# Decode attention with a parallel MLP on one core: the fourth V group is loaded by seven transfers instead of one

## The chip, the cores and the metric

The kernel runs on one core of a Trainium2 chip. The metric is the device time of one execution in microseconds (us); lower is better. Three executions of the kernel before gave 101.88, 101.95 and 102.9 us, a median of 101.95 us. One further execution was recorded by the hardware profiler.

## The reference

One decode step (one token, model width 1024) goes through two branches, whose results are added to the token:

```python
xn = layernorm(x)                                  # 1 x 1024
# branch A: attention over the last W = 4096 positions
q = xn @ wq                                        # 32 heads of 128; wq is 1024 x 4096
k = k_cache[:, :, Sk - W:, :]                      # 4 groups of 4096 x 128, 8 query heads each
v = v_cache[:, :, Sk - W:, :]
p = softmax(q . k * 128 ** -0.5)
A = (p . v) @ wo                                   # wo is 4096 x 1024
# branch B: MLP
h = gelu_tanh(layernorm(xn) @ w1 + b1)             # w1 is 1024 x 3584
B = h @ w2 + b2                                    # w2 is 3584 x 1024
out = x + A + B
```

Everything is bf16. Each weight and each cached position is used for one token only, so the core has to bring in some 40 MB and does little arithmetic on each byte.

## The kernel before

The program is written with one instruction stream for each engine and explicit semaphores; no scheduler changes the order. All bulk loads are issued by the SP queue in the order of the source: four transfers of wq (2 MB each, into the tile WA), four of w1 (1.75 MB each, into the tile W1, which the profile calls W), four of K and four of V (1 MB each, one for each group, into the tile KV). Then SP waits until TensorE has read all of w1 (line 304), and issues four transfers of w2 into the place of w1 and seven of wo into the place of wq (line 140, in `load_rows`; the sizes are in `W2_CHUNKS` and `WO_CHUNKS`). ACT issues three loads of one row each at the start (x, b1 and b2).

Each bulk transfer covers all 128 partitions. In a V transfer (line 192) partition m of group g receives the positions 32 m to 32 m + 31, which lie next to each other in memory: one row of 32 x 128 bf16 elements, 8 KB. The transfer raises the semaphore `s_v[g]` by 16 when all its data has landed.

TensorE works through the stages in the order in which the data arrives: the q projection (line 267), the first MLP layer (line 282), transposes of K (line 360), scores (line 382), softmax with DVE and ACT, the first nine row blocks of w2 (line 422), then probabilities times V (line 445), the rest of w2, and wo (line 422 again, called from line 471). Ahead of line 445 it waits for all four V groups (line 442). After each wo transfer but the first and the last, some matmuls without use are run (line 473). The last wo matmul releases the copy on ACT (line 477) and the output write (line 479).

Of the kernel before, what the change touches and what calls it, by code (L numbers as in the profile page):

```python
# [13 lines left out]
DH = 128  # L14
REP = HQ // HKV
SK = 65536
W = 4096
NBLK = W // 128
# [4 lines left out]
W1_CHUNKS = [2, 2, 2, 2]  # L23
W2_CHUNKS = [9, 9, 8, 2]
WO_CHUNKS = [8, 8, 8, 4, 2, 1, 1]
KEEP_BUSY = [[], [512] * 6, [512] * 2, [512], [256], [256], []]
PAD = 32

# [13 lines left out]
def bass_parallel_sum__sliding_block_cached__mixer_channel_mlp__decode_kernel(  # L42
# [18 lines left out]
    pe, dve, act, pool, sp = nc.tensor, nc.vector, nc.scalar, nc.gpsimd, nc.sync  # L61

    def sems(name, n):
        return [nc.alloc_semaphore(f"{name}{i}") for i in range(n)]
# [5 lines left out]
    s_v = sems("s_v", HKV)  # L70
    s_wo = sems("s_wo", len(WO_CHUNKS))
    s_w2 = sems("s_w2", len(W2_CHUNKS))
# [46 lines left out]
    V = KV[:, HKV * W: HKV * W + HKV * NBLK * DH]  # L119
# [17 lines left out]
    def load_rows(dst, src, chunks, width, semaphores):  # L137
        c0 = 0
        for j, n in enumerate(chunks):
            sp.dma_start(  # L140
                dst[:, c0 * width:(c0 + n) * width].rearrange("p (c n) -> p c n", c=n),
                src[:, c0:c0 + n, :],
            ).then_inc(semaphores[j], 16)
            c0 += n
# [44 lines left out]
            A_k_cache[0, g, SK - W:SK, :].rearrange("(m b) d -> m (b d)", m=128),  # L189
        ).then_inc(s_k[g], 16)  # L190
    for g in range(HKV):
        sp.dma_start(
            V[:, g * NBLK * DH:(g + 1) * NBLK * DH],
            A_v_cache[0, g, SK - W:SK, :].rearrange("(m b) d -> m (b d)", m=128),
        ).then_inc(s_v[g], 16)


    def stats(src, ms, veps):
# [106 lines left out]
    load_rows(W2, w2_p, W2_CHUNKS, D, s_w2)  # L305
    load_rows(WA, wo_p, WO_CHUNKS, D, s_wo)

# [36 lines left out]
    for u in range(NUNIT):  # L344
        g, hu = u // 2, u % 2
# [71 lines left out]
    def out_rows_mms(weights, vec, chunks, semaphores, j, stop_at=None):  # L417
        c0 = sum(chunks[:j])
        pe.wait_ge(semaphores[j], 16)
        for c in range(c0, c0 + chunks[j]):  # L420
            for a in range(4):
                ins = pe.matmul(acc(a), lhsT=vec[:, c:c + 32],  # L422
                                rhs=weights[:, c * D + a * 256: c * D + (a + 1) * 256],
                                start=False, stop=(c == stop_at))
        return ins
# [13 lines left out]
    pe.wait_ge(ACT.sem, C["exp"])  # L439
    wait_kt(pe, 5)  # L440
    for g in range(HKV):
        pe.wait_ge(s_v[g], 16)
    V4 = V.rearrange("p (g b d) -> p g b d", g=HKV, b=NBLK)
    for b in range(NBLK):
        last = pe.matmul(PS[0:32, 4 * 512:5 * 512], lhsT=Pb[:, b * HQ:(b + 1) * HQ], rhs=V4[:, :, b, :],  # L445
# [23 lines left out]
    pe.wait_ge(DVE.sem, C["OT"])  # L469
    for j in range(len(WO_CHUNKS)):  # L470
        last = out_rows_mms(WA, OT, WO_CHUNKS, s_wo, j, stop_at=31)
        for n in KEEP_BUSY[j]:
            pe.matmul(PS[0:32, 0:n], lhsT=OT[:, 0:32], rhs=WA[:, 0:n])  # L473
# [37 lines left out]
```

## Time and profile before

| What | Value |
|---|---|
| median of three executions | 101.95 us |
| the profiled execution | 101.74 us |
| its span, from first to last instruction | 100.5 us |
| outside the span | 1.24 us |
| bytes moved, mean rate | 39.94 MB, 397 GB/s |
| TensorE matmuls busy | 70.4 us |
| DVE, ACT, GpSimd busy | 21.4, 12.0, 3.1 us |

The span is what the trace covers; the time of an execution has about 1.2 us more. The page cuts the span into 40 slices of 2.5 us. A digit for an engine or for the DMA is its busy share in tenths, with 9 for 90% or more. The core has 16 DMA engines; this text calls what one of them has to do for the SP queue a ring. Every row of a transfer is a packet in the trace, with its start, its duration and its size, and each ring ends its part of a transfer with a packet of 4 bytes that counts the semaphore up. The trace also has the moment of each such count, here called a landing mark: 16 marks for each 128-row transfer.

### The profile page before, as it was taken

The numbers are of one execution on the slowest core, as the hardware profiler recorded it, in microseconds if no ns is written. First come the engines' busy times: TensorE is split into PE (matmuls) and PEld (weight loads), VectorE is DVE, ScalarE is ACT, GpSimd is POOL, SyncE is SP. The second block draws the span as 40 slices with busy tenths as digits, with TensorE's granted clock in tenths as the row PEclk, the third lists the DMA queues.
The fourth block names the chain that finished last, engine by engine and source line by source line (L and its number), as shares of the span: only waits on it lengthen the run. The fifth ranks groups of instructions, "written<-read, shape, count | busy, mean of one in ns | idle before, by whom it ended". The sixth has DMA issues, their size and how long they took to land.

```text
span 100.5 us, 1606 instructions
## 1 busy us (share of the span) xinstructions
PE 70.4 (70%) x727; PEld 37.9 (38%) x727; DVE 21.4 (21%) x48; ACT 12.0 (12%) x15; POOL 3.1 (3%) x18
## 2 busy tenths in 40 slices
PE   0439999999795729576999856049997507098761
PEld 1322224344232213226999842035444404061430
DVE  0453000000200000029869344540005100000000
ACT  2206000000000000025547400400000000000001
POOL 6600000000000000000000000000000000000000
PEclk9999999999999999999999985555999996555899
DMA  4899999999999999999999999999999999999940
GB/s 105 352 441 450 424 417 424 430 431 428 439 417 412 428 445 399 423 427 421 421 417 414 424 437 451 433 404 445 407 409 445 417 430 437 430 417 395 397 154 1
DMA packets 3907, 39.94 MB, mean 397 GB/s; under 512 B 439, under 2 KB 443, under 8 KB 958
## 3 DMA queue, kind: packets, MB, share of 16 engines
q1 hardware_dynamic: 3896, 39.85, 94.6%
q8 instruction: 5, 0.08, 0.3%
q10 hardware_dynamic: 6, 0.01, 0.0%
HBM read 39.86 MB, written 0.00 MB: 397 GB/s over the span
## 4 chain that ended last, share of the span: by engine, by line
DMA 67%; SPq 26%; PE 4%; issue 1%; ACT 0%
DMA W<-in_B_w_dram 37%; DMA WA<-in_A_wo_dram 30%; SPq L140 26%; PE PS L282 3%; ACT ORow L477 0%; PE PS L422 0%; PE PS L291 0%
## 5 line engine op out<-in xcount | busy, mean ns | idle before, releaser
L267 PE MATMUL PS<-WA,XNZ 128*8 128x512 bf16 x64 | 16.4, 424 | 0.0
L282 PE MATMUL PS<-W,YTb 128*1 128x512 bf16 x56 | 12.7, 379 | 5.0 <-DMA W<-in_B_w_dram 5.0
L422 PE MATMUL PS<-WA,OT 128*32 128x256 bf16 x128 | 6.7, 355 | 8.6 <-DMA WA<-in_A_wo_dram 8.5
L267 PEld LDWEIGHTS PS<-WA,XNZ 128*8 128x8 bf16 x64 | 6.0, 94 | 10.8 <-issue 4.3
L282 PEld LDWEIGHTS PS<-W,YTb 128*1 128x1 bf16 x56 | 4.4, 83 | 13.4 <-DMA W<-in_B_w_dram 6.0
L422 PEld LDWEIGHTS PS<-WA,OT 128*32 128x32 bf16 x128 | 3.9, 121 | 12.3 <-DMA WA<-in_A_wo_dram 7.8
L360 PE MATMUL PS<-identb,KV 128*128 128x128 bf16 x128 | 7.5, 219 | 1.3 <-ACT ROW L295 1.3
L422 PE MATMUL PS<-W,GT 128*32 128x256 bf16 x112 | 5.2, 321 | 4.1 <-DMA W<-in_B_w_dram 4.1
L360 PEld LDWEIGHTS PS<-identb,KV 128*128 128x128 bf16 x128 | 7.2, 98 | 1.5 <-ACT ROW L295 1.4
L445 PE MATMUL PS<-KV,Pb 128*32 128x512 bf16 x32 | 7.6, 398 | 0.0
L367 DVE COPY KV<-PS 128x1024 bf16<-128x1024 bf16 x10 | 6.3, 686 | 0.6 <-PE PS L360 0.6
L372 ACT ACTIVATE KV<-PS 128x1024 bf16<-128x1024 bf16 x6 | 5.8, 1019 | 1.9 <-PE PS L360 1.9
L297 DVE CAST ROW<-PS 1x2048 bf16<-1x2048 f32 x1 | 2.3, 2278 | 17.1 <-PE PS L282 17.1
L295 ACT ACTIVATE ROW<-PS 1x1536 bf16<-1x1536 f32 x1 | 1.4, 1439 | 34.6 <-PE PS L282 34.6
L422 PEld LDWEIGHTS PS<-W,GT 128*32 128x32 bf16 x112 | 3.5, 110 | 5.2 <-DVE SUMP L409 4.6
L445 PEld LDWEIGHTS PS<-KV,Pb 128*32 128x32 bf16 x32 | 3.2, 102 | 4.0 <-issue 0.8
L274 DVE CAST Q<-PS 8x512 bf16<-8x512 f32 x1 | 0.7, 679 | 17.8 <-PE PS L267 17.8
L477 ACT ACTIVATE ORow<-PS 128x256 bf16<-128x256 f32 x1 | 0.4, 383 | 33.8 <-PE PS L422 33.8
L473 PE MATMUL PS<-WA,OT 128*32 128x512 bf16 (+1 forms) x11 | 4.3, 499 | 0.0
L382 PE MATMUL PS<-QT,KV 128*128 128x8 bf16 x128 | 3.4, 166 | 0.4 <-DVE KV L367 0.4
L382 PEld LDWEIGHTS PS<-QT,KV 128*128 128x128 bf16 x128 | 3.3, 96 | 0.6 <-DVE KV L367 0.6
L259 PE MATMUL PS<-ROW,oneb 1*1 1x512 bf16 x7 | 3.1, 619 | 0.0
(85 smaller groups left out, 34.0 us busy)
## 6 DMA issues: line engine op xcount, KB each, us to landing
WA<-in_A_wq_dram SPq DMA_DIRECT2D x4, 2048.0 KB, 14.0
W<-in_B_w_dram SPq DMA_DIRECT2D x4, 1792.0 KB, 30.6
WA<-in_A_wo_dram SPq DMA_DIRECT2D x3, 2048.0 KB, 39.1
W<-in_B_w_dram SPq DMA_DIRECT2D x2, 2304.0 KB, 24.7
KV<-in_A_k_cache_dram SPq DMA_DIRECT2D x4, 1024.0 KB, 39.4
KV<-in_A_v_cache_dram SPq DMA_DIRECT2D x4, 1024.0 KB, 34.1
W<-in_B_w_dram SPq DMA_DIRECT2D x1, 2048.0 KB, 31.7
WA<-in_A_wo_dram SPq DMA_DIRECT2D x1, 1024.0 KB, 42.2
```

The costliest lines, as they stand in the source:

```text
L140: sp.dma_start(dst[:, c0 * width:(c0 + n) * width].rearrange("p (c n) -> p c n", c=n), src[:, c0:c0 + n, :],).then_inc(semaphores[j], 16)
L259: pe.matmul(PS[0:1, t * 512:(t + 1) * 512], lhsT=oneb[:, :], rhs=B1R[:, t * 512:(t + 1) * 512], start=True, stop=False)
L267: last = pe.matmul(PS[0:8, 7 * 512:8 * 512], lhsT=XNZ[:, 15 * k + 7 - t:15 * k + 15 - t], rhs=WA[:, k * NQ + t * 512: k * NQ + (t + 1) * 512],
L282: last = pe.matmul(PS[0:1, t * 512:(t + 1) * 512], lhsT=YTb[:, k:k + 1], rhs=W1[:, k * F + t * 512: k * F + (t + 1) * 512], start=False, s ...
L297: C["d_hrow"] = DVE.mark(dve.tensor_copy(Hrow[:, 1536:F], PS[0:1, 1536:F]))
L360: last = pe.matmul(PSb[:, o:o + 128], lhsT=KT[:, col + bb * 128: col + (bb + 1) * 128], rhs=identb[:, :], is_transpose=True)
L367: C["dkt"][u] = DVE.mark(dve.tensor_copy(KT[:, col + 1024 * s: col + 1024 * (s + 1)], PSb[:, bk * 1024:(bk + 1) * 1024]))
L372: C["akt"][u] = ACT.mark(act.activation(out=KT[:, col + 1024: col + 2048], in_=PSb[:, bk * 1024:(bk + 1) * 1024], func=ACTF.Copy))
L382: last = pe.matmul(PS[:, b * HQ + g * REP: b * HQ + (g + 1) * REP], lhsT=KT[:, g * W + b * 128: g * W + (b + 1) * 128], rhs=QT[:, g * 8:(g ...
L422: ins = pe.matmul(acc(a), lhsT=vec[:, c:c + 32], rhs=weights[:, c * D + a * 256: c * D + (a + 1) * 256], start=False, stop=(c == stop_at))
L445: last = pe.matmul(PS[0:32, 4 * 512:5 * 512], lhsT=Pb[:, b * HQ:(b + 1) * HQ], rhs=V4[:, :, b, :], start=(b == 0), stop=(b == NBLK - 1))
L473: pe.matmul(PS[0:32, 0:n], lhsT=OT[:, 0:32], rhs=WA[:, 0:n])
```

## The change

The fourth V group is brought in by seven transfers, and the wait of TensorE ahead of line 445 counts the semaphore up to 16 for each transfer of the group (112 for the fourth, 16 for the others as before). The seven cover the 128 partitions once: 64 rows (every second partition from 0), 32 rows (every fourth from 1), 16 rows (every eighth from 3), then the partitions 7, 15, ... 127, in three transfers of five rows and one of one row. The place in the SP queue, the other groups, all destinations and all arithmetic are the same.

```diff
+V_ALL = [(0, 128, 1)]
+V_CUT = [(0, 128, 2), (1, 128, 4), (3, 128, 8), (7, 47, 8), (47, 87, 8), (87, 127, 8), (127, 128, 1)]
+V_ROWS = [V_ALL, V_ALL, V_ALL, V_CUT]
...
     for g in range(HKV):
-        sp.dma_start(
-            V[:, g * NBLK * DH:(g + 1) * NBLK * DH],
-            A_v_cache[0, g, SK - W:SK, :].rearrange("(m b) d -> m (b d)", m=128),
-        ).then_inc(s_v[g], 16)
+        v_rows = A_v_cache[0, g, SK - W:SK, :].rearrange("(m b) d -> m (b d)", m=128)
+        for lo, hi, step in V_ROWS[g]:
+            sp.dma_start(
+                V[lo:hi:step, g * NBLK * DH:(g + 1) * NBLK * DH], v_rows[lo:hi:step, :],
+            ).then_inc(s_v[g], 16)
...
     for g in range(HKV):
-        pe.wait_ge(s_v[g], 16)
+        pe.wait_ge(s_v[g], 16 * len(V_ROWS[g]))
```

## The prediction

> **What bounds the kernel.** I read the page's slices first, to see which resource is never idle.
>
> ```profile
> PE   0439999999795729576999856049997507098761
> DMA  4899999999999999999999999999999999999940
> DMA packets 3907, 39.94 MB, mean 397 GB/s; under 512 B 439, under 2 KB 443, under 8 KB 958
> q1 hardware_dynamic: 3896, 39.85, 94.6%
> q8 instruction: 5, 0.08, 0.3%
> q10 hardware_dynamic: 6, 0.01, 0.0%
> DMA W<-in_B_w_dram 37%; DMA WA<-in_A_wo_dram 30%; SPq L140 26%; PE PS L282 3%; ACT ORow L477 0%; PE PS L422 0%; PE PS L291 0%
> L422 PE MATMUL PS<-WA,OT 128*32 128x256 bf16 x128 | 6.7, 355 | 8.6 <-DMA WA<-in_A_wo_dram 8.5
> ```
>
> The DMA row is full from the third slice to the last but two, while TensorE has holes; in the last line TensorE waits 8.5 us for wo. So the end is set by the last byte of wo. The chain of waits, in order of time, gives the moments:
>
> ```profile
> 56.04 11.66 SPq L140
> 67.70 0.04 issue
> 67.75 30.27 DMA WA<-in_A_wo_dram
> 98.02 0.04 issue
> 98.06 0.32 PE PS L422 x4
> 98.41 0.38 ACT ORow L477
> ```
>
> The last wo transfer lands at 98.02, and 2.47 us follow it up to 100.49 (a matmul block, the copy, the write), which the change does not touch. The 26% that the chain puts on SP's issue is no bound: the next view, the timeline of SP, shows the last bulk issue over at 46.85 + 25.28 = 72.13, well ahead of its data.
>
> ```profile
> 17.42 16.45 SPq L192 DMA_DIRECT2D KV<-in_A_v_cache_dram  x4
> 44.52 2.29 SPq L140 DMA_DIRECT2D W<-in_B_w_dram  x4
> 46.85 25.28 SPq L140 DMA_DIRECT2D WA<-in_A_wo_dram  x7
> ```
>
> A transfer lands when the slowest of its 16 rings has finished, so I read the landing marks of the last one. They are not together: ten rings have 96.27 to 96.65, one has 96.82, and five have 97.78 to 98.02. The end therefore hangs on **five late rings**, 1.4 us behind the rest. They became late one by one: a single late mark in w1's third transfer (36.97 beside a median of 35.40), two in the second V group, five in the third wo transfer. The five instruction packets of q8 start at 31.17, 52.97, 59.83, 71.29 and 87.19 and take 1.02 to 1.08 each; each makes one ring late. The ring at 96.82 is another: its 0.3 us is there from the start, where the three one-row loads of q10 run (the first wq transfer has 15 marks up to 8.01 and one at 8.36).
>
> **The change part by part.** *Removed and added rows.* A V row is a packet of 8 KB that takes 309 to 312 ns; I take 310, and 9 ns for a 4-byte packet. The fourth group now costs every ring 8 x 310 + 9 = 2.49 us. How are fewer rows shared out? The output write of four rows has four data packets of 512 B and four landing marks of rings; a one-row load has one data packet and one. So five rows can use at most five rings, one row one ring. 64, 32 and 16 rows can use 16 rings with 4, 2 and 1 rows each. I take this, and that the small transfers begin at the same first ring each time; the one late mark that the three one-row loads leave together speaks for that. Then:
>
> - eleven rings have 7 rows and 3 counts: 7 x 310 + 27 = 2.20 us, 0.29 less than before;
> - four rings have 10 rows and 6 counts: 10 x 310 + 54 = 3.15 us, 0.66 more;
> - the first ring has 11 rows and 7 counts: 11 x 310 + 63 = 3.47 us, 0.98 more.
>
> [...]
>
> *What follows at the end.* Nothing behind V waits between the rings, so the differences stay until the last wo mark. The ten ordinary marks become at most 96.65 + 0.66 = 97.31. The ring of the one-row loads is the first ring: 96.82 + 0.98 = 97.80. The five late ones, if they lie among the eleven, become 98.02 - 0.29 = 97.73. The last of these is 97.80, 0.22 ahead of 98.02.
>
> *Price of a row in the small transfers.* No transfer of before writes a part of the partitions with a step, and none has rings that write where other rings write in a full transfer. Below I set 310 ns, as in full transfers; above 620, two packets one after the other on a shared way (the nearest row is a V-sized packet at 53.97 that met an instruction packet and took 856). I take 310, since full rows of 2, 4, 8, 14, 16 and 18 KB all run at 24 to 27 bytes per ns and ring, whatever their target. A gain over 310 is excluded: the same bytes never ran faster.
>
> [...]
>
> *Six more issues on SP* (the seven replace one). An issue that waits for nothing takes about 0.43 us there, those of V 3.7 to 4.6 because the queue is full. At 0.43 the six take 2.6 us, inside SP's idle time from 33.9 to 44.5. At 4.1 each they would take 25 us and pass it, so that the w2 issue begins near 58.5 instead of 44.5. Its data starts at 58.87 and an issue at 0.80 had its first packet at 1.82, so at the worst 0.7 us is lost. But the first nine issues of the run took 0.39 to 0.53 each and the tenth 3.52: an issue stalls only behind some nine queued transfers, so data remains in front. I take 0, ends 0 and 0.7. The w2 and wo issues queued behind have no other reader in a hurry: the last wo issue is over at 72.14, and the first 2 KB packet starts at 94.46.
>
> *TensorE's wait for 112* is hidden. The fourth group's last mark is 61.13; line 445 starts at 68.76, after the first w2 part (last mark 66.63), which is queued behind V. Even 4 us more keeps V first in the queue; without that cover, each late us would count once.
>
> *Sum:* -0.22 on the way to the last mark, 0 elsewhere: the profiled 101.74 becomes 101.52. The profiled run was 0.21 under the median of the runs, so the forecast is 101.95 - 0.22 = **101.73 us**. Since about 1% (1.0 us) is what a measurement of this kernel can tell from no change, this is "within 1%".
>
> **Rivals.** *Late rings under the small transfers.* If one of the five late rings is among the four that get 10 rows, its mark becomes 97.78 to 98.02 + 0.66 = 98.44 to 98.68, the end 0.4 to 0.7 later: **102.6** at the upper end. For it: the trace does not name rings. Against: the five instruction packets hit five different rings, as if taken in turn, and of the 11 runs of five neighbours that leave out the first ring, 7 leave out the next four as well.
>
> *Shared way of writing, the slower side.* One mechanism: in the seven transfers two rings write into one place at a time. If only the 16-row transfer and the single rows suffer, the first ring has 6 x 310 + 5 x 620 + 63 = 5.02, 2.53 more: its mark is 99.35 and the end 1.33 later, 103.3. If all rows do, 11 x 620 + 63 = 6.88, 4.39 more: 101.21, 3.19 later, 105.1. I price it at the middle, **104.2**. It decides above 1% when the first ring's rows take (98.02 + 1.02 - 96.82 + 2.49 - 0.06) / 11 = 0.42 us on average. For it: the full transfers leave the rings no spare time. Against: nothing in the trace shows two rings in each other's way.
>
> *The change doesn't shift the load.* If the small transfers take the rings in turn, 5 + 5 + 5 + 1 gives each ring one row, 8 as before, and a few counts more: +0.04, **102.0**. Against: the single late mark of the three one-row loads.
>
> *A dry queue* from the issues: +0.7 - 0.2, **102.5**.
>
> **How the numbers follow.** Forecast 0.38; late rings 0.17; shared way 0.36; no shift 0.05; dry queue 0.04. Faster by over 1% needs a loss of 1 us at the end, and the lightest ring only gains 0.29: 0.03 for what I don't see. Slower by over 1% is the shared way with most of its chance, 0.34, and 0.03 from sums of the others: 0.37. The rest, 0.60, is within 1%. The range begins at 101.4 (the five late rings' full 0.29, and the scatter of the runs) and reaches to 104.3, into the shared way's middle; the forecast with the other small cases alone has 101.4 to 102.7.
>
> **What the next profile would show.** Right: 4-byte packets of q1 grow from 436 by 16 + 16 + 5 + 5 + 5 + 1 = 48, landing marks of the last wo transfer with the five late ones 0.29 earlier and the first ring's near 97.8, V packets of 310 ns. The prediction is wrong if packets of the seven transfers take 420 ns or more, if a late mark moves 0.66 back, or if the DMA row has a hole near 60 us.

## The result, and the profile after

The changed kernel takes 102.89 us (median of ten runs, 102.76 to 103.46), the kernel before 101.88 us in the same comparison. The ratio is 1.0098, with an interval of 1.0078 to 1.0119: about 1.0 us slower. The forecast was 101.73 us, 0.2% faster. The range (101.4 to 104.3) holds the result; the direction was wrong.

The page after, the same rows as before. Its lines are numbered three to five higher (`load_rows` is line 143, the V loads line 197, the weight rows of w2 and wo line 426).

```profile
PE   0439999999896647759998934029999637088561
...
DMA  4999999999999999999999999999999999999940
GB/s 98 394 423 420 426 413 445 452 408 446 401 429 430 446 407 405 429 420 429 423 416 407 429 280 379 428 450 403 422 408 423 447 445 432 413 407 420 391 190 1
DMA packets 3955, 39.94 MB, mean 393 GB/s; under 512 B 487, under 2 KB 491, under 8 KB 1006
...
q1 hardware_dynamic: 3944, 39.85, 94.8%
q8 instruction: 5, 0.08, 0.3%
...
L426 PE MATMUL PS<-WA,OT 128*32 128x256 bf16 x128 | 6.5, 347 | 7.4 <-DMA WA<-in_A_wo_dram 7.3
```

The GB/s row of the page before, for comparison:

```profile
GB/s 105 352 441 450 424 417 424 430 431 428 439 417 412 428 445 399 423 427 421 421 417 414 424 437 451 433 404 445 407 409 445 417 430 437 430 417 395 397 154 1
```

The DMA engines are as busy as before, and the bytes are the same. What is new is in the GB/s row: the 24th slice, which begins at 58.4 us, has 280 (before 437), and the next has 379 (before 451). A busy share cannot show this, since a packet that is held up counts as busy (in the stretch shown next it is 1.07, before 1.03). The packets are 48 more, as predicted. TensorE waits no longer for wo than before (7.3 us, before 8.5): what it lost lies earlier, ahead of the first part of w2 (5.3 us, before 4.1).

The same by stretches of time: 58 to 63 us, in which the fourth V group and the first w2 transfer come in, and the rest. The last number is GB/s, the one ahead of it the DMA engines' busy share. First the kernel before, then the changed one.

```profile
58.00:63.00 5.00, 2.67 (x55) 1.74 (x51) 2.59 (x5) 0.00 (x0) 0.00 (x0) 0.66 1.03 434
63.00:98.00 35.00, 21.79 (x285) 12.01 (x285) 4.51 (x6) 1.02 (x1) 0.00 (x0) 0.76 0.96 402
```

```profile
58.00:63.00 5.00, 2.55 (x50) 1.62 (x47) 2.71 (x5) 0.00 (x0) 0.00 (x0) 0.70 1.07 343
63.00:98.00 35.00, 22.26 (x279) 12.10 (x280) 4.40 (x6) 1.02 (x1) 0.00 (x0) 0.70 0.98 414
```

Five us at 343 instead of 434 GB/s are 0.455 MB that did not move; at 434 GB/s that is 1.05 us, the whole loss. Behind 63 us nothing is lost. The chain of waits and SP's timeline agree: the last wo transfer lands 1.03 later than before (99.05, before 98.02), and the issues end early as before.

```profile
68.08 30.96 DMA WA<-in_A_wo_dram
99.05 0.04 issue
99.09 0.32 PE PS L426 x4
```

```profile
...
17.41 24.38 SPq L197 DMA_DIRECT2D KV<-in_A_v_cache_dram  x10
44.41 3.33 SPq L143 DMA_DIRECT2D W<-in_B_w_dram  x4
47.79 25.19 SPq L143 DMA_DIRECT2D WA<-in_A_wo_dram  x7
```

The packets of that stretch tell which ones were slow. The trace does not name rings, but each packet starts where the one before it on its ring ends (in the kernel before, the earliest marks of the four K transfers and the first V transfer, 41.98 to 51.92 us, stand 2.48 to 2.49 us apart, the length of eight packets of some 310 ns and one of 9), and the 4-byte packets part the transfers, so the rows can be followed. Between 54.3 and 58.5 us V packets take 309 to 340 ns, nearly as in full transfers; most rows of the 16-row transfer start there. All 23 V packets that start from 58.6 to 60.2 take 485 to 678 ns. Fifteen of them are single rows (485 to 593 ns), one is a row of the 16-row transfer, and seven are rows of the 64-row and 32-row transfers on the two rings that were already late then; the longest, 678 ns, is one of these. The 18 KB rows of w2 that start from 58.6 to 60.2 take 1.07 to 1.29 us instead of 0.69, and they belong to an ordinary transfer of 128 rows. So from 58.6 us on rows of every transfer under way are held up, and not only those of the small ones.

### The profile page after: what moved, and what is told of

Its sections match the earlier page's. It is cut to its first block, busy times and chain, and to the rows that moved or that the text cites. A ratio compares the mean times of both kernels' runs of the same rounds, so it can differ in the third digit from the quotient of the medians.

```text
span 101.5 us, 1612 instructions
## 1 busy us (share of the span) xinstructions
PE 71.8 (71%) x727; PEld 38.2 (38%) x727; DVE 21.2 (21%) x48; ACT 12.0 (12%) x15; POOL 3.2 (3%) x18
## 4 chain that ended last, share of the span: by engine, by line
DMA 67%; SPq 26%; PE 4%; issue 1%; ACT 0%
DMA W<-in_B_w_dram 36%; DMA WA<-in_A_wo_dram 30%; SPq L143 26%; PE PS L286 3%; ACT ORow L481 0%; PE PS L426 0%; PE PS L295 0%
## 5 line engine op out<-in xcount | busy, mean ns | idle before, releaser
L449 PE MATMUL PS<-KV,Pb 128*32 128x512 bf16 x32 | 9.0, 450 | 0.0
```

## The experiments

Three accounts were at hand. **A:** rows are merely dealt out to the wrong rings. **B:** a row that a ring writes into partitions that another ring writes in a full transfer shares a way with it, and both are slow (no trace names the partitions of a packet or a way, so this is the author's account of the numbers). **C:** every small transfer has a price of its own. Later **D:** the small transfers read badly, in rows of memory at a pitch of 64 KB.

**Which rings are late.** Fifteen tiny transfers of 1 to 15 rows behind the last wo transfer, in both kernels; in the changed one each of the seven transfers has its own semaphore too. (Here and below the cuts of code leave out the semaphores of added transfers and the waits for them at the end.)

```diff
+    for k in range(1, 16):
+        sp.dma_start(CEN[0:k, 32 * k - 32:32 * k], A_wo[0:k, 0:32]).then_inc(s_cen[k - 1], 16)
```

> The kernel before, with 15 tiny transfers of 1, 2, ... 15 rows of 64 bytes queued behind the last wo transfer, each with a semaphore of its own. A transfer of k rows uses k rings, so what is new in its landing marks beside those of k - 1 rows is the mark of ring k, and shows how late that ring is at the end. Theory A (late rings under the small transfers: the load is dealt out by rings and late rings are among those that got more rows): one or more of the five marks that are about 1.4 us late appear at k = 2 to 5. Theory B (shared way of writing): it leaves this open; if all five late marks appear at k = 6 or later, A falls. The first ring is expected 0.3 late in both.

> The changed kernel with a semaphore for each of the seven transfers and the same 15 tiny transfers at the end. Theory A: the rings 2 to 5 are 0.66 us later than in the kernel before, the first 0.98, the other eleven 0.29 earlier. Theory B: rings 1 to 5 are later by 1.3 to 2.5 us, and others, into whose partitions the 16-row and the single rows go, are later too, by 0.3 to 1 us, instead of earlier. Both expect about the time of the changed kernel, 102.9 us, or up to 0.3 more for the tiny transfers.

Measured: 101.84 and 103.19 us, one run each. The marks nest as expected: those of k rows are those of k - 1 rows some 0.19 later, and one new one. So each mark of the last wo transfer can be given to a ring:

| Ring | Last wo mark, before | after | moved by | row counts alone |
|---|---|---|---|---|
| 1 | 96.90 | 98.94 | +2.0 | +0.98 |
| 2 to 5 | 96.30 to 96.63 | 98.16 to 98.46 | +1.8 to +1.9 | +0.66 |
| 6, 7, 10, 11, 12 | 97.82 to 98.12 | 98.86 to 99.14 | +0.8 to +1.0 | -0.29 |
| 8, 9, 13 to 16 | 96.36 to 96.70 | 97.25 to 97.66 | +0.8 to +1.1 | -0.29 |

The five late rings are 6, 7, 10, 11 and 12. None is among those that got more rows, so A falls. The shift of rows took place as counted: the rings 2 to 5 moved about 0.9 more than the last eleven, where the counts say 0.95. But on top of it **every ring lost 1.1 to 1.4 us**. The sizes are about those that B gave: 1.3 to 2.5 us later for the rings 1 to 5, and 0.3 to 1 later for others instead of earlier. The last mark is that of ring 12, a late ring, which the prediction had gaining 0.29.

**Even numbers of rows.** Two cuts that give each ring eight rows again.

```diff
-V_CUT = [(0, 128, 2), (1, 128, 4), (3, 128, 8), (7, 47, 8), (47, 87, 8), (87, 127, 8), (127, 128, 1)]
+V_CUT = [(0, 128, 2), (1, 128, 4), (3, 128, 4)]                  # 64, 32, 32 rows
+V_CUT = [(0, 128, 2), (1, 128, 4), (3, 128, 8), (7, 128, 8)]     # 64, 32, 16, 16 rows
```

> Fourth V group by three transfers of 64, 32 and 32 rows (steps 2, 4 and 4; the last from partition 3): every ring has 8 rows again, no single rows. Theory A: no ring has more rows, so the time of before, 101.9 us (plus 0.02 for two more counts). Theory B, if only rows of the 16-row and single-row transfers share a way: also 101.9; if any step in the partitions makes rings share: 2.4 us more for these eight rows at 620 ns, 104.3. Theory C (each small transfer has a cost of its own to begin): 101.9 plus two such costs; the change's 1.0 us over six added transfers would be 0.17 each, so 102.2.

> Fourth V group by four transfers of 64, 32, 16 and 16 rows (steps 2, 4, 8 and 8, the last two from partitions 3 and 7): every ring has 8 rows, no single rows, but two transfers of 16 rows. Theory A: 101.9 us. Theory B: in each 16-row transfer two rings share a way, so that a row takes some 620 ns instead of 310: twice 0.31 more on all rings, 102.5. Theory C: three added transfers at 0.17, 102.4; B and C are told apart by the packets, which take 310 ns by C and some 500 to 620 by B.

Measured: 64, 32 and 32 rows have a ratio of 0.9998 (0.9976 to 1.0021), no change. With 64, 32, 16 and 16 rows it is 1.011 (1.0077 to 1.0143), 1.1 us and as much as the change itself, without any ring having more rows. The stretches of the first, then of the second:

```profile
58.00:63.00 5.00, 2.52 (x49) 1.59 (x46) 2.74 (x5) 0.00 (x0) 0.00 (x0) 0.64 1.05 442
```

```profile
58.00:63.00 5.00, 2.64 (x54) 1.71 (x51) 2.62 (x5) 0.00 (x0) 0.00 (x0) 0.74 1.06 359
```

442 beside 359 GB/s: cutting a transfer up and stepping over partitions cost nothing with 64 and 32 rows, whose V packets stay at 309 to 326 ns; two transfers of 16 rows do cost. That each ring keeps to its own partitions in the first cut and not in the second is B's reading; the trace does not name the partitions of a packet. The size was off: 0.62 had been expected from two rows at double time.

**Double dose.** The 16-row transfer is cut into 5, 5, 5 and 1 rows as well.

```diff
+V_CUT = [(0, 128, 2), (1, 128, 4), (3, 43, 8), (43, 83, 8), (83, 123, 8), (123, 124, 1), (7, 47, 8), (47, 87, 8), (87, 127, 8), (127, 128, 1)]
```

> The changed kernel with the 16-row transfer of step 8 also cut into 5 + 5 + 5 + 1 rows: 64, 32 and twice 5, 5, 5, 1. Now 11 rings have 6 rows and 5 or 6 have 12 to 14. By counts of rows alone the first ring, at 96.9 in the kernel before, would have 14 x 0.31 - 2.49 = 1.9 more, 98.8, so the end is 0.75 us later than before: 102.7. [...]

Measured: 103.89 us, ratio 1.0207 (1.0191 to 1.0224), 2.1 us over before, and 1.2 above what the counts of rows give (102.7).

**Where the rows are written, where they are read.** Back to the kernel before, with 384 KB more behind the fourth V group, into a scratch tile with 3 KB in each partition: by one transfer of 128 rows, or by eight of 16 rows, with the target or the source in two arrangements.

```diff
+    EX = sb("EX", [128, 1536], bf16)
+    sp.dma_start(EX[:, :], v_rows[:, 0:1536])                                  # one of 128 rows
+    for n in range(8):                                                         # eight of 16 rows:
+        sp.dma_start(EX[n:128:8, :], v_rows[n:128:8, 0:1536])                  # every eighth partition
+        sp.dma_start(EX[16 * n:16 * n + 16, :], v_rows[n:128:8, 0:1536])       # 16 neighbours
+        sp.dma_start(EX[n:128:8, :], v_rows[16 * n:16 * n + 16, 0:1536])       # every eighth, rows of memory neighbours
```

> The kernel before with 384 KB more: one transfer of 128 rows of 3 KB into a scratch tile, queued behind the fourth V group. It is the measure for the next two. Each ring gets 8 rows of some 0.12 us: about 1.0 us more than before (102.9), packets of some 120 ns, whatever the theory.

> The same 384 KB from the same memory rows into the same scratch tile, by eight transfers of 16 rows (every eighth partition). Theory B (two rings share a way into the partitions): rows take twice as long, 2.0 us more than before, 103.9. Theory C (each small transfer has a cost of its own, about 0.55 us after the kernel with two 16-row transfers): 1.0 + 8 x 0.55, 106.3, with packets of 120 ns and gaps between them. Theory D (the reading of 16 memory rows at a pitch of 64 KB is slow, wherever they go): the same time as the next one.

> Like the one with eight transfers of 16 rows, with the same memory rows in each transfer, but into 16 neighbouring partitions instead of every eighth. [...] Theories C and D: the same time as with every eighth partition.

> The kernel with eight 16-row transfers into every eighth partition, but each reads 16 neighbouring rows of memory (pitch 8 KB) instead of every eighth (64 KB). Theory D: now as fast as one transfer of 128 rows, 103.1. Theories B and C: as before with 64 KB, 104.6.

> The kernel with eight 16-row transfers into blocks of 16 neighbouring partitions, with the blocks in the order 0, 2, 4, 6, 1, 3, 5, 7 instead of 0 to 7; everything else the same. [...] Theory C (price for each small transfer) and theory D (reading at a pitch of 64 KB is slow): no change by the order, 104.7.

| Extra 384 KB | Ratio to before (interval) |
|---|---|
| one transfer of 128 rows | 1.0149 (1.0103 to 1.0195) |
| eight of 16 rows, every eighth partition | 1.0274 (1.0257 to 1.0291) |
| the same, neighbouring rows of memory | 1.0269 (1.0251 to 1.0286) |
| eight of 16 rows, 16 neighbouring partitions | 1.027 (1.0232 to 1.0307) |
| the same, blocks in the order 0, 2, 4, 6, 1, 3, 5, 7 | 1.0301 (1.0262 to 1.034) |

The one transfer of 128 rows already cost 1.5 us instead of the 1.0 expected. The source makes no difference, so D falls. C falls too: eight times 0.55 us would have been 106.3, and the packets themselves grow, from 121 ns in the 128-row transfer to some 240 in the 16-row ones. B's estimate for every eighth partition (103.9) was too low by 0.7, part of which lies in the 128-row transfer already. That blocks of 16 neighbours cost more than every eighth partition was the author's estimate, and no run shows it (1.027 beside 1.0274). The order of blocks is not settled by the times, since the intervals overlap. In the packets of the changed order the early blocks reach 416 ns, 3.4 times 121, and most later ones fall back to 210 to 260; in the order 0 to 7 nearly all stay under 250. The author's explanation, that the rings spread over several transfers and then meet less, is argued, not shown by a run of its own.

**The same transfers, 64 partitions higher.** Eight transfers of five rows of 3 KB use rings 1 to 5 and write the partitions 0 to 19 and 32 to 51, each transfer with a step of four; in the other kernel only the partitions differ, by 64. Which rings write the one or the other set in a full transfer no trace shows.

```diff
+    for n in range(8):
+        p = 0 + 32 * (n // 4) + n % 4      # 64 + ... in the other kernel
+        sp.dma_start(EX[p:p + 20:4, :], v_rows[n:n + 40:8, 0:1536])
```

> The kernel before with eight more transfers of five rows of 3 KB into a scratch tile behind the fourth V group: 24 KB more on each of the rings 1 to 5, as three rows of 8 KB in the change. [...] Theory B: no ring meets another; the first ring has 8 x 0.13 = 1.03 more and stays ahead of the late rings (96.9 + 1.03 = 97.9 beside 98.0): 101.9, no change. Theory C (price for each transfer): 0.17 each or more, 1.4 us on the rings 1 to 5 beside the 1.03: 99.3 on the first, 103.2. Theory D (pitch of 64 KB): as the next kernel.

> [...] By counts of rows alone, and by C and D: the time of the kernel with the partitions 0 to 51.

Measured: partitions 0 to 51 1.0005 (0.999 to 1.0021); 64 higher 1.0116 (1.0073 to 1.016). Same rings, same bytes, same memory rows, same number of transfers. First the rate with the partitions 0 to 51, then 64 higher:

```profile
58.00:63.00 5.00, 2.79 (x58) 1.86 (x54) 2.47 (x5) 0.00 (x0) 0.00 (x0) 0.51 1.05 436
```

```profile
58.00:63.00 5.00, 2.56 (x51) 1.64 (x47) 2.70 (x5) 0.00 (x0) 0.00 (x0) 0.73 1.05 359
```

With the partitions 0 to 51 all 40 packets take 121 ns. With those 64 higher they rise to 245, and the first w2 rows to 1.34 us. The time is 102.78, 0.9 over before. No mark of the first w2 transfer lies before 65.75, where with the partitions 0 to 51 the eight earliest lie from 64.84 to 65.20: taken in order, all 16 marks are 0.73 to 1.05 later. So rings that had nothing added are delayed too. For the same rows on the same rings, then, the time depended on the partitions they were written into. That agrees with B. Which rings meet was not shown, nor that in the partitions 0 to 51 none do.

**One ring alone, 64 partitions higher.** To see whether others are held up, the first ring alone writes 24 KB, into the partitions 0 to 3 and 32 to 35 or into those 64 higher.

```diff
+        sp.dma_start(EX[p:p + 1, :], v_rows[n:n + 1, 0:1536])      # p as above
```

> [...] The first ring has 8 x 0.13 = 1.0 more, 97.9 at the end, still ahead of the late rings: no change, 101.9; the other 15 rings' marks of the first w2 transfer as before (64.9 to 65.2 but for the three late ones).

> [...] If a contested way holds up every ring: all marks of the first w2 transfer move back together, by up to 1.0, the late ones too, and the time is 102.3 to 102.9.

Measured: partitions 0 to 35 1.001 (0.9992 to 1.0028), 64 higher 1.0034 (1.002 to 1.0049), about 0.3 us over before. The two intervals just overlap, so the times alone hardly tell the two apart; the spans do (100.4 to 100.8 us, and 100.8 to 101.1 with the higher ones), and so do the packets. First the stretch with the partitions 0 to 35, then 64 higher:

```profile
58.00:63.00 5.00, 2.67 (x55) 1.74 (x52) 2.59 (x5) 0.00 (x0) 0.00 (x0) 0.68 1.03 433
```

```profile
58.00:63.00 5.00, 2.78 (x59) 1.85 (x56) 2.48 (x5) 0.00 (x0) 0.00 (x0) 0.72 1.02 415
```

The rate of the stretch falls from 433 to 415 GB/s. On the writing ring the last 3 KB packets take 232 to 240 ns instead of 121. At the same time one other ring, which has nothing added, has two w2 rows of 1.12 and 1.10 us instead of 0.69, and one mark of the first w2 transfer stands alone at 65.83: a second ring is held up. Which one it is the trace does not name. A price of these partitions for the writing ring alone would not show on a second one. The last wo mark is 98.34 (98.08 with the partitions 0 to 35), on one ring alone (the next has 98.15); that it is the first ring was supposed and not shown. The other rings hardly move: eleven marks of the first w2 transfer lie from 64.92 to 65.20, beside 64.86 to 65.24 for the twelve earliest of before. Yet at 59.6 to 59.9 some w2 rows that had taken 686 to 694 ns take 720 to 729, on one ring after another. So here mainly two rings were slowed, and the others a little. With five rings writing 64 partitions higher (the pair of runs above) the earliest mark of that transfer is 65.75 instead of 64.84, and with the whole change all rings lost over 1.1. How the small hold grows into a loss on all rings stays open.

## Why the prediction was wrong

- **What bounds the kernel:** right. The last wo mark sets the end, and what was lost at 58 to 63 us came out undiminished at 99.05. TensorE's wait for the four V groups and the six issues cost nothing: the issues took 0.42 to 4.6 us each and ended at 41.8, inside SP's idle time.
- **How rows are dealt out:** right, with 48 more counts, k rows on k rings, always from the first ring (the nested marks show it), and none of the late rings among the first five. The last was partly luck: it had been argued from five neighbours hit in turn, and the late rings are 6, 7, 10, 11 and 12. The shift between the two sets of rings is there, about 0.9 us for 0.95.
- **The price of a row:** this step failed. The forecast took 310 ns for each row of the small transfers, "since full rows of 2, 4, 8, 14, 16 and 18 KB all run at 24 to 27 bytes per ns and ring, whatever their target", and put at nothing what these rows do to other rings. All of those transfers covered 128 partitions, so they could not speak about transfers that reach only a part of them. In its place the runs showed single rows of 485 to 593 ns, and rows of other transfers held up beside them: 1.07 to 1.29 us for a w2 row of 0.69. The first ring moved 2.0 us back where 0.98 was counted. The late rings, which set the end, moved 0.8 to 1.0 back where 0.29 forward was counted: 99.05 instead of 97.73. For 64 and 32 rows without the small transfers the price held (0.9998).
- **The signs of being wrong:** of the three named, two came, packets of 420 ns and more and late marks over 0.66 back; the DMA row has no hole near 60 us.
- **The rival with a shared way** was right that rows of the small transfers take longer than 310 ns (485 to 678 ns) and hold others up, with the wrong reach; the shared way itself is its explanation, and no trace names one. That only the 16-row transfer and the single rows suffer, its lower case, no run had shown; then 64 and 32 rows cost nothing (0.9998) and two transfers of 16 rows did (1.011). It charged only the rings that write the rows and made the first ring the last one, with 103.3 at the least. In fact every ring lost 1.1 to 1.4 us; rings 1 to 5 had room for their extra rows, and a late ring stayed last. The eleven rows of the one ring with four single rows took about 0.40 us on average, under the 0.42 at which the rival was to decide above 1%. The price of 104.2 was 1.3 too high, and the chance of 0.36 was too low: no transfer into a part of the partitions had tested the 310 ns of the forecast. The range holds the result only because this rival stretched it: without it the range ended at 102.7.
- **The other rivals:** no late ring lies among the first five; the load does shift; the queue does not run dry.

The gain by row counts was small, 0.29 us on eleven rings, and it agrees with the shift of about 0.9 us between the two sets. It was paid for by 1.1 to 1.4 us of held-up writing on every ring.

## What to carry to other kernels

In this load-bound kernel cutting a transfer up was free for 64 and 32 rows at a step (0.9998), and added transfers of five rows were free in the partitions 0 to 51 (1.0005). It was not free for 16 rows (1.011), nor were the five rows free 64 partitions higher (1.0116). Moving rows to less busy rings took 0.29 us off eleven rings by the counts, and slowed all 16 by 1.1 to 1.4; that their rows then go into other rings' partitions is the author's account: before dealing work out anew by its amount, measure its rows in the places where they then go. When a busy row is full on both sides of a comparison, read the GB/s of the same slices: a held-up packet is busy too (1.07 at 343 GB/s here, beside 1.03 at 434).

## What was not expected of the hardware

- The slow rows also delayed rings that had nothing added: with five rings writing 64 partitions higher, all 16 marks of the first w2 transfer came 0.73 to 1.05 us later. In the change itself ring 9, for one, with 0.29 us less to do, moved 0.89 us back; which rows met its own the trace does not tell.
- Sixteen neighbouring partitions cost no more than sixteen spread ones (1.027 and 1.0274).
- The landing marks of small transfers that follow each other on a ring came no closer than about 0.19 us here, for rows of 64 bytes and of 3 KB alike, although 3 KB packets started every 0.125 us.
